# A marker transfer ahead of the last value piece, and a key load held back until it lands

## The chip, the cores and the metric

One core of a Trainium2 chip runs the kernel. The metric is the device time in microseconds (us). The profiled span is some 2 us shorter than the time. "Engine" means two things below: TensorE, VectorE and so on compute, and sixteen **DMA engines** move the data. A **landing** is the moment at which the last of a transfer's sixteen semaphore updates arrives; each DMA engine sends one.

## The reference

Two attention blocks for one decoded token, with their outputs side by side. Block A looks at the whole cache of 8192 tokens, block B at the last 2048.

```python
q = (x @ wq).reshape(B, Sq, Hq, Dh).transpose(0, 2, 1, 3)   # B=4, Sq=1, Hq=32, Dh=128
k = jnp.repeat(k_cache, rep, axis=1)                        # 8 kv heads, rep = 4
v = jnp.repeat(v_cache, rep, axis=1)                        # block B: cache[:, :, Sk - W:, :]
scores = jnp.einsum("bhqd,bhkd->bhqk", q, k) * (Dh ** -0.5)
p = softmax(scores)
o = jnp.einsum("bhqk,bhkd->bhqd", p, v)
return o.transpose(0, 2, 1, 3).reshape(B, Sq, Hq * Dh) @ wo
...
return jnp.concatenate([a, b], axis=-1)
```

The kernel has to read 184.6 MB, nearly all of it keys and values, and computes little with each byte.

## The kernel before

The work is cut into 20 units: 0 to 3 are the batches of block B, 4 to 19 are pairs of heads of block A. A unit needs 4 MB of keys and 4 MB of values, each in one of two buffers. SyncE issues nearly all loads, in program order, on one queue. Before each load it waits until the buffer is free:

```python
def kv_load(kind, u):
    ...
    if un["P"] == 1:                       # block B: keys in 2 pieces, values in NSEG = 4 pieces of 1 MB
        for q in range(NPART[kind]):
            if kind == "K":
                w = [("T", tjob_idx[(u - 2, 8 * q + 7)])] if u >= 2 else []
            else:
                w = [("otr", u - 2)] if u >= 2 else ...
            ...
            op("sp", dma(buf[:, slot, q * n:(q + 1) * n, :], src), waits=w, inc=(...))
        return
    w = [("otr", u - 2)] if kind == "V" else [("otr", u - 3)] if u >= 2 * T0P else [("T", tjob_idx[(u - 2, NJ - 1)])]
    ...                                    # block A: 4 MB in one transfer
    op("sp", lambda sp: sp.sem_inc(sem, bump), waits=w, bump=(sem, bump, None))
    op("sp", dma(buf[:, slot, :, :].rearrange("p t d -> p (t d)"), src), inc=(kind, u, 0))

kv_load("K", 0)
for u in range(1, NU + 1):
    if u < NU:
        kv_load("K", u)
    kv_load("V", u - 1)
    ...                                    # and 1 MB of output weights, from u = 6 on at every even u
for i, n in enumerate(WCH):                # eight last pieces of output weights, 128 KB each
    ...
```

So the queue holds, in order, K4, V3 (four pieces), K5, V4, K6, V5 and so on, "K5" being the keys of unit 5. TensorE's program is a part ahead of a loop, a loop of ten turns over two units each, and a tail for the last values and weights. TensorE's instructions are themselves fetched from memory in blocks.

## Time and profile before

| what | value | from |
|---|---|---|
| time | 439.17 us (439.14 to 439.53) | runs of the kernel before |
| profiled span | 437.0 us | page, first line |
| DMA queue of SyncE | 99.1% of the 16 engines' time | page, part 3 |
| TensorE busy | 84% | page, part 1 |
| VectorE, ScalarE busy | 48%, 45% | page, part 1 |
| K5: issued, landed | 98.80, 122.61 us | timeline, and the trace's semaphore updates |
| last landing | 434.43 us | trace's semaphore updates |

The full DMA row is the thing to read first: busy shares of computing engines say little in a kernel whose queue never runs empty. The lines stand in the prediction.

### The profile page before, as it was taken

The page shows a single profiled execution, that of the slowest core. Times are in us where ns is not written, and L with a number is a line of the kernel's source. Part 1 is how long each engine was busy: PE and PEld are TensorE (multiplying, and loading weights), DVE is VectorE, ACT ScalarE, POOL GpSimd, SP SyncE. Part 2 cuts the span into 40 slices and gives each one's busy share as a digit, 9 for nine tenths or more (in the row PEclk, how much of TensorE's full clock was granted, in tenths as well). Part 3 has the DMA queues.
Part 4 walks back from the last instruction along what each step waited for, and adds up shares of the span by engine and source line. Part 5 has one row for each costly group of instructions (what it writes and reads, how often), then busy time and mean ns, then how long its engine had stood idle before and what let it go on. Part 6 is the DMA issues. An engine that isn't in the chain of part 4 may idle for free.

```text
span 437.0 us, 15525 instructions
## 1 busy us (share of the span) xinstructions
PE 365.0 (84%) x7174; PEld 337.9 (77%) x7184; DVE 210.0 (48%) x406; ACT 195.0 (45%) x249; POOL 27.7 (6%) x88
## 2 busy tenths in 40 slices
PE   0168898998998959895989598969868996989996
PEld 0158897997997949795979588868868886979975
DVE  0004455664564634563456247525643563455651
ACT  1024473573653625371634254434534462536530
POOL 6100000000000000000000000000100000000000
PEclk9999999999999988999999899989996999799999
DMA  8999999999999999999999999999999999999996
GB/s 340 430 421 421 429 412 430 418 439 412 445 432 432 424 438 432 432 432 432 432 432 429 432 432 430 431 433 432 410 454 432 432 432 432 432 432 411 447 407 255
DMA packets 10996, 184.73 MB, mean 423 GB/s; under 512 B 1236, under 2 KB 2280, under 8 KB 2408
## 3 DMA queue, kind: packets, MB, share of 16 engines
q1 hardware_dynamic: 10960, 184.56, 99.1%
q8 instruction: 8, 0.13, 0.1%
q14 instruction: 4, 0.03, 0.0%
q10 hardware_dynamic: 24, 0.01, 0.0%
HBM read 184.56 MB, written 0.01 MB: 422 GB/s over the span
## 4 chain that ended last, share of the span: by engine, by line
PE 54%; DMA 40%; issue 2%; DVE 1%; SPq 1%; ACT 1%
DMA K_sb<-in_A_k_cache_dram 29%; PE KT L283 27%; PE OT L338 11%; DMA K_sb<-in_B_k_cache_dram 7%; PE SB L322 5%; PE SA L322 4%; DMA V_sb<-in_A_v_cache_dram 4%; PE KT L396 4%; PE SA L350 1%; PE KT L338 1%; SPq L566 1%; DVE oacc L404 1%; PE KT L263 1%; ACT KT_sb L299 1%; DVE OS L501 0%
## 5 line engine op out<-in xcount | busy, mean ns | idle before, releaser
L283 PE MATMUL KT<-identf,K_sb 128*128 128x128 f32 x1280 | 207.6, 296 | 44.1 <-DMA K_sb<-in_A_k_cache_dram 30.7
L299 ACT ACTIVATE KT_sb<-KT 128x1024 bf16<-128x1024 bf16 (+1 forms) x192 | 165.1, 881 | 120.6 <-PE KT L283 120.6
L283 PEld LDWEIGHTS KT<-identf,K_sb 128*128 128x128 f32 x1280 | 147.6, 150 | 49.3 <-DMA K_sb<-in_A_k_cache_dram 31.7
L299 DVE COPY KT_sb<-KT 128x512 int32<-128x512 int32 x160 | 110.5, 691 | 132.1 <-PE KT L283 130.7
L338 PE MATMUL OT<-PT,V_sb 128*128 128x64 bf16 x2560 | 78.1, 193 | 1.6 <-issue 1.1
L338 PEld LDWEIGHTS OT<-PT,V_sb 128*128 128x128 bf16 x2560 | 75.9, 98 | 1.8 <-issue 1.2
L469 ACT ACTIVATE PT<-Dt 128x512 bf16<-128x512 f32 x40 | 24.6, 630 | 84.0 <-DVE Dt L458 84.0
L322 PEld LDWEIGHTS SA<-RQc,KT_sb 128*128 128x128 bf16 x1280 | 56.9, 98 | 2.3
L322 PEld LDWEIGHTS SB<-RQc,KT_sb 128*128 128x128 bf16 x1280 | 51.1, 97 | 7.9 <-issue 4.4
L322 PE MATMUL SA<-RQc,KT_sb 128*128 128x16 bf16 x1280 | 56.4, 170 | 0.0
L322 PE MATMUL SB<-RQc,KT_sb 128*128 128x16 bf16 x1280 | 52.9, 170 | 0.0
L420 DVE TENSOR_REDUCE M<-SB 128x8 f32<-128x512 f32 (+1 forms) x20 | 13.8, 692 | 50.0 <-PE SB L322 50.0
L441 POOL PARTITION_ALL_REDUCE MB<-M1m x20 | 7.7, 387 | 334.3 <-DVE M1m L434 334.3
L396 PE MATMUL KT<-Wo_sb,OL 128*4 128x512 bf16 x80 | 18.9, 379 | 0.0
L201 PE MATMUL KT<-ident,x_sb 4*128 4x4 bf16 x8 | 0.6, 170 | 19.9 <-POOL identf L537 19.9
L201 PEld LDWEIGHTS KT<-ident,x_sb 4*128 4x128 bf16 x8 | 0.4, 112 | 20.1 <-issue 20.1
L476 DVE TENSOR_REDUCE LB<-SA 128x8 f32<-128x512 f32 (+1 forms) x20 | 13.7, 684 | 2.8 <-PE SA L350 2.8
L458 DVE TENSOR_TENSOR Dt<-SA,MBm 128x512 f32<-128x512 f32 x20 | 13.8, 692 | 0.7
L367 DVE TENSOR_TENSOR ORx<-KT,MSK 32x1024 bf16<-32x1024 bf16 x10 | 12.1, 1211 | 3.3 <-PE KT L362 3.3
L458 DVE TENSOR_TENSOR Dt<-SB,MBm 128x512 f32<-128x512 f32 x20 | 13.6, 681 | 0.0
L420 DVE TENSOR_REDUCE M<-SA 128x8 f32<-128x512 f32 (+1 forms) x20 | 13.6, 681 | 0.0
L350 PE MATMUL SA<-PT,onesb 128*128 128x128 bf16 x168 | 12.7, 218 | 0.0
(69 smaller groups left out, 118.0 us busy)
## 6 DMA issues: line engine op xcount, KB each, us to landing
K_sb<-in_A_k_cache_dram SPq DMA_DIRECT2D x15, 4096.0 KB, 22.5
V_sb<-in_A_v_cache_dram SPq DMA_DIRECT2D x15, 4096.0 KB, 30.3
K_sb<-in_B_k_cache_dram SPq DMA_DIRECT2D x8, 2048.0 KB, 23.6
V_sb<-in_B_v_cache_dram SPq DMA_DIRECT2D x16, 1024.0 KB, 18.4
V_sb<-in_B_wq_dram SPq DMA_DIRECT2D x1, 4096.0 KB, 12.5
V_sb<-in_A_wq_dram SPq DMA_DIRECT2D x1, 4096.0 KB, 21.8
Wo_sb<-in_B_wo_dram SPq DMA_DIRECT2D x4, 1024.0 KB, 11.9
K_sb<-in_A_k_cache_dram SPq DMA_DIRECT2D x2, 2048.0 KB, 17.5
```

What stands on the lines that cost most here:

```text
L283: ins = pe.transpose(out=bkf[:, pi * 128:(pi + 1) * 128], in_=K_sbf[:, slot, t0:t0 + 2, :].rearrange("p t d -> p (t d)"), identity=identf[ ...
L299: ins = e.tensor_copy(out=d, in_=r) if eng == "dve" else e.activation(out=d, in_=r, func=ACTF.Copy)
L322: ins = pe.matmul(out=stb[:, t % NTH * C:(t % NTH + 2) * C], lhsT=ktv[:, pi, :, e], rhs=RQc[:, u % 2, t // TS, e, :], start=(e == 0), stop ...
L338: ins = pe.matmul(out=otb[:, s * NW:s * NW + w], lhsT=V_sb[:, slot, t, :], rhs=PT[:, slot, t * C:t * C + w], start=(j == 0), stop=(j == n ...
L350: ins = pe.matmul(out=SA[u % 2][:, s * NM:(s + 1) * NM], lhsT=onesb[:, :], rhs=PT[:, u % 2, c0:c0 + NM], start=(i == 0), stop=(i == n - 1))
L367: return dve.tensor_tensor(out=ORx[:, :, :, :], in0=bk[0:NR, 0:128].rearrange("p (i o r) -> p r o i", o=1, r=C).broadcast_to([NR, C, C, 12 ...
L396: ins = pe.matmul(out=bk[0:Bn, 0:D], lhsT=OL[:, i, :], rhs=Wo_sb[:, i, :], start=(i == 0), stop=(i == C - 1))
L420: return dve.tensor_reduce(out=M1[:, h * n:(h + 1) * n].rearrange("p (s h) -> p s h", h=C), in_=bank[:, :].rearrange("p (s j h) -> p s h j ...
L441: return pool.partition_all_reduce(MB[:, 0:n], M1m[:, 0:n], channels=128, reduce_op=ReduceOp.max)
L458: return dve.tensor_tensor(out=Dt[:, h * NTH * C:(h + 1) * NTH * C].rearrange("p (s j h) -> p s j h", s=Sh, h=C), in0=bank[:, :].rearrange ...
L469: return act.activation(out=PT[:, u % 2, a:b], in_=Dt[:, a:b], func=ACTF.Exp, scale=scale)
L476: return dve.tensor_reduce(out=LB[:, 0:n].rearrange("p (s h) -> p s h", h=C), in_=SA[u % 2][:, 0:NSEG * NM].rearrange("p (s j h) -> p s h ...
```

## The change

A transfer that has fully passed a point of the queue can be noticed if a tiny transfer, a marker, is placed there and its semaphore is watched. The change puts such a marker (16 rows of 64 bytes, so one row for each DMA engine) ahead of the last piece of V3 and lets SyncE hold K5 back until the marker has landed. The queue then stays short at this point: K5 joins it when 1 MB is left. The values of a unit have semaphores that TensorE counts down itself, which SyncE therefore cannot watch; this explains the detour by a marker.

```diff
+        rs_sb = sb("rs_sb", [16, 32], BF16)
...
+        MARKS = (3,)
+        marked = []
+
+        def mark(u):
+            if u in MARKS:
+                op("sp", dma(rs_sb[:, :], WO[0][0:16, 0:32]), inc=("rs", u))
+                marked.append(u)
+
+        def passed():
+            return [("rs", marked.pop())] if marked else []
...
                     if kind == "K":
-                        w = [("T", tjob_idx[(u - 2, 8 * q + 7)])] if u >= 2 else []
+                        w = ([("T", tjob_idx[(u - 2, 8 * q + 7)])] if u >= 2 else []) + passed()
                     else:
                         w = [("otr", u - 2)] if u >= 2 else ...
+                        if q == NSEG - 1:
+                            mark(u)
...
-            op("sp", dma(buf[:, slot, :, :]..., src), inc=(kind, u, 0))
+            op("sp", dma(buf[:, slot, :, :]..., src), waits=passed() if kind == "K" else [], inc=(kind, u, 0))
...
             if u % 2 == 0 and tn in pieces:
                 P, q = pieces[tn]
+                mark(u - 1)
```

(The diff is cut: the new semaphore's name is also added to two lists.) With `MARKS = (3,)` the last hunk does nothing.

More of the change, by code (lines that the diff above doesn't have):

```diff
@@ L128, in bass_concat_heads__gqa_block_cached__sliding_block_cached__decode_kernel @@
                  "out0", "out1", "out2", "Tq", "Td", "Ta", "S", "PV", "Ed", "Ea", "Eq", "vs", "sub", "exp", "otr", "otp",
-                 "ocp", "Ef", "fin0", "fin1", "ar1", "SM", "msk", "pset", "setup", "pm0", "pm1", "oc", "ocB", "mkb", "perm", "rq"]
+                 "ocp", "Ef", "fin0", "fin1", "ar1", "SM", "msk", "pset", "setup", "pm0", "pm1", "oc", "ocB", "mkb", "perm", "rq", "rs"]
         sems = {n: sm("s_" + n) for n in names}
@@ L160, in sem_of @@
             return sems["vs" if t in ("max", "maxc", "sum", "rcp", "os") else t]
-        DMA_KEYS = ("K", "Kh", "KH", "V", "Vh", "VL", "WL", "x", "out", "WQ", "wo")
+        DMA_KEYS = ("K", "Kh", "KH", "V", "Vh", "VL", "WL", "x", "out", "WQ", "wo", "rs")
         plan = {e: [] for e in ("sp", "pe", "act", "dve", "pool")}
@@ L747, in kv_load @@
                 return
-            op("sp", dma(buf[:, slot, :, :].rearrange("p t d -> p (t d)"), src), inc=(kind, u, 0))
+            op("sp", dma(buf[:, slot, :, :].rearrange("p t d -> p (t d)"), src), waits=passed() if kind == "K" else [], inc=(kind, u, 0))
         for P in (1, 0):
```

## The prediction

> **What bounds the kernel now.** I read the page first (digits, queues, chain), then the SyncE timeline, the landings of single transfers, the chain in the last ten microseconds and the DMA view of short stretches. The page:
>
> ```profile
> DMA  8999999999999999999999999999999999999996
> GB/s 340 430 421 421 429 412 430 418 439 412 445 432 432 424 438 432 432 432 432 432 432 429 432 432 430 431 433 432 410 454 432 432 432 432 432 432 411 447 407 255
> ...
> q1 hardware_dynamic: 10960, 184.56, 99.1%
> ```
>
> The DMA row is full from the first slice to the last, and SyncE's queue q1 alone takes 99.1% of the time of the 16 engines. TensorE is busy for 84%, but it often waits for keys. So the transfers set the end. The steady rate is 4.19 MB in 9.71 us (spacing of landings in the trace), or 432 GB/s. SyncE's timeline around the change:
>
> ```profile
> 83.26 0.53 SPq L566 DMA_DIRECT2D K_sb<-in_A_k_cache_dram  x1
> 89.09 2.53 SPq L566 DMA_DIRECT2D V_sb<-in_B_v_cache_dram  x4
> 98.80 0.54 SPq L566 DMA_DIRECT2D K_sb<-in_A_k_cache_dram  x1
> 105.95 0.54 SPq L566 DMA_DIRECT2D V_sb<-in_A_v_cache_dram  x1
> 123.99 0.54 SPq L566 DMA_DIRECT2D K_sb<-in_A_k_cache_dram  x1
> ```
>
> These are the keys of unit 4, the four value pieces of unit 3, the keys of unit 5 (the load that the change holds back), the values of unit 4, and the keys of unit 6. The single load at 98.80, by its line:
>
> ```profile
> L566 SPq DMA_DIRECT2D K_sb<-in_A_k_cache_dram x1: 535/535/535, 98.8 to 98.8; - x1
> ...
> DMA to landing us min/median/max: 23.8/23.8/23.8
> ```
>
> It lands at 98.8 + 23.8 = 122.6, though its data need only 9.7 us: it stands 14 us in the queue. The four value pieces land at 105.44, 107.92, 110.41 and 112.89 (each time the last of 16 semaphore updates), and 112.89 + 9.72 = 122.61. There is no gap between these transfers.
>
> **The engines do not finish together.** I took the 16 updates of each transfer, as each engine sends one. At 112.89 the engines lead the slowest one by 2.07, 2.01, 1.73, 1.59, 1.38, 1.36, 1.29, 0.57, 0.41, 0.39, 0.35, 0.32, 0.26, 0.11, 0.08 and 0 us. The list hardly changes to the end: each engine runs at its own limit (a 32 KB packet takes 1.21 us, 27 GB/s), so a lead once made stays. The leads come from small jobs that one engine gets and the others don't:
>
> ```profile
> q8 instruction: 7, 0.11, 0.8%
> q14 instruction: 1, 0.01, 0.0%
> ```
>
> That is the DMA view from 20 to 75 us: seven 16 KB and one 8 KB fetches of instructions, each on one engine; another 8 KB one comes at 90.9. Nine leads are below 0.6 and seven above 1.2, which fits nine engines hit once and seven not yet. Three fetches follow later, at 159.8, 289.1 and 431.3 us. In the leads they show as one engine each: 1.31 became 0.66, about 2.05 became 1.41, and 1.63 became 0.21. All three hit engines that had a large lead, so none delayed a landing. This is what I think the change spoils.
>
> The last fetch, 431 to 433 us, and the end of the chain:
>
> ```profile
> q8 instruction: 1, 0.02, 3.5%
> ```
>
> ```profile
> 433.83 0.11 PE KT L700
> ...
> 434.43 0.11 PE SA L700
> 434.54 0.21 PE KT L700
> 434.74 0.12 PE SA L700
> 434.87 0.02 issue
> 434.89 0.41 DVE osb L704
> ```
>
> The last weight piece lands at 434.43; after that come two matmuls, a copy and the store, 2.6 us to the end of the span at 437.0. A later last landing moves the end one for one.
>
> **What the Trainium skill says.** "DMA: Bandwidth & Descriptors", Queues, rings and completion order, says that on each engine descriptors are consumed in ring order and that the semaphore increment lands only after the earlier writes of that engine. So a marker over 16 rows, one on each engine, passes an engine when it has done the first three value pieces, and its full count arrives with the slowest engine. The trace agrees: the updates of one transfer spread over the same 2.07 us that the engines are apart. The same page, Latency and other measured facts, gives about 600 ns to the first byte of such a load. In this trace the first load is issued at 0.80, its instruction takes 0.39, and its first packets start between 1.84 and 2.23, some 1.04 to 1.43 us after the issue; those first packets take 1.69 to 2.23 instead of 1.21. I use the trace. "Runtime: NRT & Kernel Launch", Instruction fetch mechanics, says the sequencer fetches 16 KiB blocks on its own DMA queue and calls the cost mostly hidden. The trace has such 16,384-byte packets on q8, but each takes about 1.05 us from one engine that carries data too.
>
> **The change part by part.**
>
> 1. It adds one transfer of 16 rows of 64 bytes. On each engine that is one packet and one semaphore write. In the trace 1 KB packets take about 46 ns and semaphore packets 9 ns, with a gap of 6: about 0.06 us on every engine, the slowest included. SyncE spends about 0.35 us more to issue it (the output stores take 0.29 to 0.37), at 91 us, 18 us before the queue needs anything: hidden. No buffer of the computation is touched.
>
> 2. It moves the key load of unit 5 from 98.80 to the marker's landing. That is 110.41 + 0.06 = 110.47; SyncE answers a semaphore about 0.02 us later (89.07 to 89.09), so about 110.5. The value load of unit 4 goes to 111.1 instead of 105.95; its turn in the queue is at 122.6, so nothing is lost. The keys of unit 6 keep their own release at 123.9. Later loads are issued 15 to 20 us ahead: unchanged.
>
> 3. When the key load is issued, the slowest engine has one piece of 1 MB before it, 2.48 us, until 112.9 + 0.06. The new packets are there at 111.5 to 111.9; so it should not run dry, or hardly. The engines with leads over about 1.3 are done with the piece at 110.9 to 111.7 and wait. To be running at full pace, an engine needs issue + 1.04 to 1.43 and then the slow first packet, 0.5 to 1.0 longer than the steady 1.21: an effective start at 112.0 to 112.9. So the seven leads of 1.29 to 2.07 shrink to between 0 and 0.9, about 0.45 in the middle. An engine at the late edge may even become the new slowest, by 0 to 0.2 us; I count 0.05.
>
> 4. The later fetches then fall on engines without the old cushion. They cost their engines 0.65, 0.64 and 1.42 us (from the leads above). With a lead of 0.45 the first two push that engine 0.2 behind the slowest, the third nearly 1.0. Three different engines are hit, so the largest counts, not the sum: 1.42 - 0.45 = 0.97. If the leads that remain are 0.9, it is 0.5; if 0, 1.4.
>
> Sum on the last landing and so on the end: 0.06 + 0.05 + 0.97 = 1.08 us. I take off a little because that engine may be fed sooner than the cold start of the program suggests: 0.85. From 439.17 this gives **440.0 us**.
>
> **The rivals.**
>
> *A: hidden anyway.* If the new descriptors come within 0.6 us of the issue and full pace follows at once, only leads over about 1.6 shrink, and the engine of the last fetch (1.59 here) keeps enough. Only the marker is left: 439.2. For it: the figure of 600 ns. Against: 1.04 us and slow first packets in this trace.
>
> *B: the whole ring runs dry.* If the answer to the marker takes over 2.5 us, all engines stop: each further microsecond costs one. With 1.5 us of extra gap and the fetches on top: about 441.5. Against it: the first packets of the first load came after 1.04 us, even cold.
>
> *C: aligned engines help.* If the engines shared a common limit, the slow ones would catch up while the fast ones wait, up to the mean lead of about 1.0: 438.2. Against it: the steady rate is the same for leaders and laggards over 300 us, and in the last 2 us, where the leaders have finished, the packets of the others still take 46 ns.
>
> *D: TensorE becomes the bound.* The keys of unit 5 land at 122.6 in both cases, and TensorE takes them up only at 123.63, so there is even 1 us of room.
>
> **Range and chances.** The centre is my sum; A marks the lower edge and a lead of zero plus a small dry spell the upper one: 439.2 to 440.9. Two per cent is 8.8 us, far beyond anything here; only a fault in my reading of the queue could reach it. Faster 0.005, within 2% 0.985, slower 0.01.
>
> **What would show it.** In the profile after: the key load of unit 5 issued near 110.5 and landing near 122.7 (issue to landing 12 instead of 23.8); the spread between the first and last update of that landing below 1.0 us instead of 2.07, and staying small; small steps of the later landings where the fetches near 160 and 289 fall; the last landing near 435.3, and most of the delay arising after 431. The prediction is wrong if the spread stays at 2 us, if the key load lands after 123.5 (the ring ran dry), or if the end moves while the landings before 431 and the fetches after it don't account for it.

## The result, and the profile after

| | before | after |
|---|---|---|
| time, median | 439.17 us (439.14 to 439.53, 4 runs) | 441.02 us (440.80 to 441.23, 4 runs) |
| profiled span | 437.0 us | 439.0 us |

The ratio is 1.004, with a 95% interval of 1.0023 to 1.0058. A ratio here is the mean time of one kernel's fast runs over that of the other's of the same rounds, so it isn't quite the ratio of the medians. The change costs 1.85 us by the medians: within 2%, but clear of noise, and just above the predicted range of 439.2 to 440.9.

The page of the changed kernel, parts 2 and 3:

```profile
DMA  8999999999999999999999999999999999999996
GB/s 341 422 423 420 426 417 428 420 448 403 403 430 430 418 443 430 433 433 427 433 433 430 430 433 433 430 428 430 422 443 442 433 430 430 430 430 414 446 412 226
...
q1 hardware_dynamic: 10992, 184.56, 98.8%
```

The row of nines shows nothing: a gap of a few tenths of a microsecond disappears in slices of 11 us. Only the rate of the eleventh slice, 403 against 445 before, is a hint. SyncE's timeline of the changed kernel (start, duration, instruction) shows the intent carried out:

```profile
88.86 1.84 SPq L567 DMA_DIRECT2D V_sb<-in_B_v_cache_dram  x3
90.74 0.66 SPq L567 DMA_DIRECT2D rs_sb<-in_A_wo_dram  x1
91.45 0.54 SPq L567 DMA_DIRECT2D V_sb<-in_B_v_cache_dram  x1
110.80 0.54 SPq L567 DMA_DIRECT2D K_sb<-in_A_k_cache_dram  x1
111.45 0.53 SPq L567 DMA_DIRECT2D V_sb<-in_A_v_cache_dram  x1
123.77 0.53 SPq L567 DMA_DIRECT2D K_sb<-in_A_k_cache_dram  x1
```

Three pieces, the marker at 90.74, the fourth piece, and K5 at 110.80 instead of 98.80. K6 is issued as before. The line of the K5 load alone:

```profile
L567 SPq DMA_DIRECT2D K_sb<-in_A_k_cache_dram x1: 535/535/535, 110.8 to 110.8; - x1
...
DMA to landing us min/median/max: 12.5/12.5/12.5
```

It lands at 123.28. A 4 MB load that follows without a gap lands 9.72 us after its predecessor, and V3 landed at 113.05, so 10.23 us lie between them: **0.51 us are lost there**. The window of 109 to 115 us, with busy time of the engines, TensorE's granted clock, share of the DMA engines and GB/s as columns (a packet counts in the window in which it starts, hence shares above 1), first before, then after:

```profile
109.00:115.00 6.00, 6.00 (x105) 5.69 (x104) 3.89 (x7) 4.21 (x5) 0.00 (x0) 1.00 1.10 466
```

```profile
109.00:115.00 6.00, 6.00 (x104) 5.68 (x103) 3.88 (x7) 3.98 (x4) 0.00 (x0) 1.00 0.94 365
```

TensorE is busy all the six microseconds in both, while the queue moves a fifth less. Summing the packets' own times from 110 to 116 us gives 96 engine-microseconds before (all that sixteen engines have) and 84 after: 12 are lost, most of them by engines that had a lead.

I then compared every landing with its counterpart of the kernel before. The delay doesn't grow evenly; it comes in steps:

| landing | delay against before | what happens there |
|---|---|---|
| last piece of V2, 93 us | +0.14 | an 8 KB fetch at 90.7; ahead of the marker |
| last piece of V3, 113.05 | +0.16 | the marker adds no more than 0.02 |
| K5, 123.28 | +0.67 | 0.51 at the marker |
| K7, 164.88 | +0.92 | an 8 KB fetch at 162.5 |
| K17, 371.66 | +0.98 | |
| first weight piece, 433.07 | +1.02 | |
| second weight piece, 434.37 | +1.97 | a 16 KB fetch at 432.1 |
| last weight piece, 436.37 | +1.94 | |

The chain of the changed kernel at its end (start, duration, what):

```profile
411.18 23.19 DMA Wl_sb<-in_A_wo_dram
434.37 0.04 issue
434.41 0.27 PE KT L701
434.69 0.11 PE SA L701
...
436.69 0.12 PE SA L701
436.81 0.02 issue
436.84 0.41 DVE osb L705
```

Before, the two products that end the chain stood at 434.54 and 434.74, and the weight pieces were mostly there ahead of them. Now the chain runs over the second weight piece, the very landing with the step of 0.95 us. In both traces the copy that ends the chain starts 0.46 us after the last landing, so the end follows the landings one for one. The same 0.46 stands in every other trace but two, e9 and e10 below.

The leads of the engines went as expected: the spread of the sixteen updates, 2.22 us at V3, is 0.72 at K5 (2.07 before) and stays below 1.05 until 432. The fetch near 432 made it 1.94 at once.

### The profile page after: what moved, and what is told of

Read it like the earlier page. It is cut to its first block, busy times and chain, and to the rows that moved or that the text cites. A ratio compares the mean times of both kernels' runs of the same rounds, so it can differ in the third digit from the quotient of the medians.

```text
span 439.0 us, 15536 instructions
## 1 busy us (share of the span) xinstructions
PE 368.8 (84%) x7184; PEld 339.4 (77%) x7184; DVE 209.8 (48%) x406; ACT 195.0 (44%) x249; POOL 27.6 (6%) x88
## 4 chain that ended last, share of the span: by engine, by line
PE 48%; DMA 42%; PEld 4%; issue 2%; SPq 1%; DVE 1%; ACT 0%; PEldq 0%
DMA K_sb<-in_A_k_cache_dram 29%; PE KT L284 24%; PE OT L339 10%; DMA K_sb<-in_B_k_cache_dram 7%; DMA Wl_sb<-in_A_wo_dram 5%; PE SB L323 4%; PE SA L323 4%; PE KT L397 3%; PEld KT L284 2%; PE SA L351 1%; SPq L567 1%; PE KT L264 1%; PEld OT L339 1%; PEld SA L323 1%; DVE oacc L405 1%
```

## The experiments

My theory: the loss has two parts. A **dry spell**: K5 is issued so late that even the slowest DMA engine waits for it. And **lost leads**: the faster engines wait for the slowest, so that a later fetch of instructions, which takes over a microsecond from one engine, no longer falls on an engine that has time to spare. Rivals: the marker itself disturbs the queue; TensorE is the cause, at the passage from the small to the large units; or the engines are realigned once and that is all.

In each trace the fetch near 91 us hits another engine and shifts all that follows by 0 to 0.65 us, ahead of the marker. So the dry spell is measured within one trace: landing of K5, minus landing of V3, minus 9.72. In the kernel before it is 122.61 - 112.89 - 9.72 = 0.00. All kernels gave correct results unless it is said otherwise. The experiments were run in four batches, each with runs of before on its own chip: e1 to e4 (before: 439.18 us), e5 to e8 (439.17), e9 to e11 (439.21, the same chip as e5 to e8) and e12 to e14 (439.21).

### e1_marker_only: the marker, but no wait

```diff
         def passed():
-            return [("rs", marked.pop())] if marked else []
+            return []
```

> The marker stays, the key load of unit 5 does not wait for it. Theory (the loss comes from holding the key load back: a dry spell of about 0.5 us, then engines without a lead): the load is issued near 98.8 again, lands near 122.7, spread of its sixteen updates about 2 us, time 439.2 us (within 0.15 of before). Rival (the marker itself, its 64-byte packets or its semaphore, disturbs the queue): time near 441.0.

Measured: 439.24 us (438.97 to 439.61), ratio 0.9998 (0.9985 to 1.0011). Dry spell 0.00, spread at K5 2.48 us. The marker itself costs nothing that can be measured; that rival falls.

### e2_hold_t5: the wait, but no marker

```diff
 # kernel before
-op("sp", dma(buf[:, slot, :, :]..., src), inc=(kind, u, 0))
+op("sp", dma(buf[:, slot, :, :]..., src), waits=[("T", tjob_idx[(4, 5)])] if kind == "K" and u == 5 else [], inc=(kind, u, 0))
```

> No marker; the key load of unit 5 waits instead for the sixth transposition of unit 4 on TensorE, which ends near 110.5 in the trace of before, so that it is issued at about the time at which the changed kernel issues it. Theory: same loss as the change, 440.5 to 441.1, landing of the load 0.3 to 0.7 us late, spread below 1 us. Rival (the marker is the cause): 439.2.

Measured: 440.16 us (439.59 to 441.20), ratio 1.0027 (1.0015 to 1.0039). The time is below my band. The load by its line:

```profile
L566 SPq DMA_DIRECT2D K_sb<-in_A_k_cache_dram x1: 535/535/535, 110.1 to 110.1; - x1
...
DMA to landing us min/median/max: 13.1/13.1/13.1
```

It was issued at 110.10, 0.7 us earlier than in the changed kernel, while the slowest engine finished V3 0.36 us later (112.94 against 112.58). That was enough: the dry spell is 0.02, no loss at K5, against what I had expected. But most of the leads went all the same (spread at K5 1.14 us, from 2.54 at V3; I had expected below 1), and at the second weight piece, just after the fetch at 431.5, the delay against before jumps from about 0.55 to 1.34; at the last one it is 1.20. So this trace happened to separate the two parts: lost leads without a dry spell cost it about 0.65 us, and no marker is needed for it. The median of the six runs lies 1.0 us over before, but the dry spells of the five without a trace are not known.

### e3_marker_2mb and e4_marker_0mb: more and less data left behind the marker

```diff
 # e3: one piece earlier                    # e4: behind the last piece
-                        if q == NSEG - 1:
+                        if q == NSEG - 2:
                             mark(u)
 # e4: mark(u) moved from ahead of the last piece's transfer to after it
```

> The marker one piece earlier, so that 2 MB instead of 1 MB of values are behind it when the key load is issued (near 108.2). Theory: the new packets come 1.3 to 2.0 us after the issue, near 109.5 to 110.2, before the fastest engine is done at 110.8; nobody runs dry, the spread stays about 2 us, time 439.2 to 439.4. Rival (any wait for a marker costs, through the sleep of SyncE or the later value load): near 441.0, or at least 440.

> The marker behind the last value piece, so that nothing is left in the queue when the key load is issued (near 113.1). Theory: all sixteen engines run dry, the load lands 12.5 us after its issue as in the changed kernel, near 125.6, which is 2.9 us late; then the last fetch adds 0.9 to 1.3. Time 443.0 to 443.6. Rival (the loss is the realignment of the engines, which is already complete in the changed kernel): about 441 again.

Measured: e3 439.39 us (439.18 to 439.76), ratio 1.0004 (0.9991 to 1.0017); e4 443.48 us (443.10 to 443.89), ratio 1.0096 (1.0081 to 1.0110). The loads by their lines, e3 and then e4:

```profile
L567 SPq DMA_DIRECT2D K_sb<-in_A_k_cache_dram x1: 535/535/535, 108.8 to 108.8; - x1
...
DMA to landing us min/median/max: 14.4/14.4/14.4
```

```profile
L567 SPq DMA_DIRECT2D K_sb<-in_A_k_cache_dram x1: 535/535/535, 113.6 to 113.6; - x1
...
DMA to landing us min/median/max: 12.3/12.3/12.3
```

Both times are as the theory expected, though in e4 not by the expected parts: the last fetch adds 0.6 us, not 0.9 to 1.3, and an 8 KB fetch at 165.5 another 0.6. With 2 MB behind the marker nothing is lost: the dry spell is -0.02, and the spread falls only from 2.59 to 2.33 us. A wait for a marker is harmless as such. With nothing behind it the dry spell is 2.76 us and the spread 0.20: all engines stood still. In these traces I set the issue of K5 against the end of the slowest engine's last data packet of V3:

| | issue of K5 ahead of that end | dry spell | spread at K5 |
|---|---|---|---|
| e3 | 4.25 us | -0.02 | 2.33 |
| e2 | 2.84 us | 0.02 | 1.14 |
| the change | 1.78 us | 0.51 | 0.72 |
| e4 | -0.65 us | 2.76 | 0.20 |

In the last two rows the two columns add up to 2.1 to 2.3 us. That is the time such a load needs here, from its issue, until it keeps every engine fed. The six other traces with this marker and wait (e6 at its first marker, e8, e10, e11, e13, e14) give 2.0 to 2.3 as well; e5, at another place, gives 3.2. To spare the leaders too, their lead of about 2 us has to be added, as e3 nearly has.

### e5_mark15 and e6_marks4: the same at another place, and at four

```diff
-        MARKS = (3,)
+        MARKS = (15,)            # e5
+        MARKS = (3, 7, 11, 15)   # e6
```

> The same marker and wait once, but at unit 15 (ahead of the 1 MB output weights, the key load of unit 17 waits), near 360 us instead of 110. Theory: a dry spell of about 0.5 us there, the fetches near 160 and 289 still harmless because the leads are still there, the one near 431 harmful: 440.6 to 441.2. Rival (the loss belongs to the passage from the small to the large units at 110 us, where TensorE is busiest): 439.2 to 439.4.

> Markers and waits at units 3, 7, 11 and 15. Theory: every one costs its own dry spell of 0.4 to 0.6 us, for in each the slowest engine too waits for its new packets; the loss of the leads comes once. So 441.0 + 3 x 0.5 = 442.5 (442.1 to 442.9). Rival (the whole loss is one realignment, later markers find the engines already together): 441.0 to 441.3.

Measured: e5 441.20 us (440.94 to 441.45), ratio 1.0044 (1.0031 to 1.0058); e6 444.35 us (443.19 to 444.62), ratio 1.0118 (1.0103 to 1.0133). In e5 the loss is as large as in the changed kernel, though the marker stands at 360 us instead of 110; the passage between small and large units is not the cause. The fetches at 160.5 and 289.1 leave hardly a step (0.1 us at most), as expected. But the dry spell is 1.42 us instead of the expected 0.5. Some 0.6 of it is common to all engines, and one engine alone is 0.78 later than the next. No fetch lies there. The packets show that this engine falls behind right at the restart: its first packet is the last to start, 2.08 us after the issue, and takes 2.03 us, and its second takes 1.66 instead of 1.21. Why it does stays open. The fetch at 433.5 then adds only 0.5.

In e6 the measure of the dry spell gives 0.26, 0.37, 0.72 and 0.59 us at the four markers. An 8 KB fetch at 281.9 falls into the third stretch and one engine is 0.32 behind the rest at its end, so about 0.4 of the 0.72 is left for the dry spell. Each marker costs one, and the rival of a single realignment is wrong. My number was too low here as well: three more markers cost 3.3 us, not 1.5. The fetches explain a part (steps of 0.6 near 160 and 1.4 near 434 in the profiled run, which was the fastest of the four); why the other three runs were over a microsecond longer than the profiled one no trace shows.

### e7_short_before and e8_short_after: a first, failed try at the fetch

```diff
 # query projection: two of the four contraction steps left out, 256 instructions less for TensorE
-                    for c in range(DC):
+                    for c in (0, DC - 1):
                         ins = pe.matmul(out=bk[:, hl * Bn:(hl + 1) * Bn], lhsT=wv[:, c, hq * DH:(hq + 1) * DH], ...)
```

> The kernel before with two of the four contraction steps of the query projection left out (wrong result on purpose): TensorE's program has 256 instructions less, so the last 16 KB fetch, near 431 us, should be gone. Theory: in the kernel before that fetch hits an engine with a lead of 1.6 us and costs nothing, so the time stays at 439.2 (438.9 to 439.4). It is the base for the next run.

> The changed kernel with the same cut (wrong result on purpose). Theory: the step of about 0.95 us near 432 disappears with the fetch, the dry spell (0.5) and the fetch near 160 (0.25) stay: 0.7 to 1.1 us over the short kernel before, 439.9 to 440.2. Rival (the step near 432 has another cause than the fetch, such as the row of small weight loads): 1.7 to 2.0 over it, near 441.0.

Measured: e7 439.47 us (439.07 to 439.68), ratio 1.0003 (0.9989 to 1.0017); e8 441.14 us (440.96 to 441.32), ratio 1.0044 (1.0030 to 1.0058). (The wrong queries still passed the comparison with the reference.) The edit missed its aim: one of the fetches before 72 us is gone, but the one near 432 is still there, at 431.8 and 432.3. It seems that the 256 instructions were exactly one 16 KB block (64 bytes each, by this count), so that all later block boundaries stayed where they were in the program. The runs say nothing about the fetch; they only repeat the loss.

### e9_notail_before, e10_notail_after and e11_refetch_after: the boundary moved to the end

```diff
 # e9 (of before), e10 and e11 (of the change): of the last values, only 2 of every 16 products are kept
-                for i in range(TC):
+                for i in range(TC) if bank is None else (0, TC - 1):
 # e11 also: the column sums of the last unit eight times over, to bring the boundary forward again
-                for s in range(NSEG):
+                for s in list(range(NSEG)) * (8 if u == L else 1):
```

> The run before this showed that cutting the program ahead of the loop by a whole 16 KB block leaves the fetch near 432 where it was, so it told nothing of the fetch. Here TensorE's tail is cut instead: of the last value product, 2 of 16 tokens in each eighth are multiplied (wrong result on purpose), which ends the program before the next 16 KB boundary. The fetch near 432 should be gone. In the kernel before it costs nothing: 438.7 to 439.4. Base for the next two.

> The changed kernel with the same cut tail (wrong result on purpose). Theory (the last microsecond of the loss is the fetch falling on an engine without a lead): no fetch near 432, no step there; the dry spell and the 8 KB fetches remain, 0.6 to 1.2 us over the cut kernel before, about 440.0. Rival (the step near 432 comes from the row of small weight loads or from TensorE's own end): 1.7 to 2.1 over it, near 441.

> The changed kernel with the cut tail, but with the eight column-sum products of the last unit done eight times over (the same values again), so that the tail crosses the 16 KB boundary once more, with few instructions on the path. Theory: the fetch is back and with it the step of about 0.5 to 1.0 us: 440.6 to 441.3. If the cut of the products was what helped and not the fetch: as the run before.

Measured: e9 440.20 us (ratio 1.0026, 1.0012 to 1.0039), e10 441.18 (1.0046, 1.0032 to 1.0059), e11 440.76 (1.0039, 1.0025 to 1.0052). By the times this failed: the base e9 is a microsecond over before, and e11 lies below e10. The landings tell it otherwise. In e9 and e10 the fetch moved to 434.1 and 434.5, when hardly any data were left, and their delays against before show no jump of more than 0.2 us in the tail: the last landing of e10 is 435.58. In e11 the fetch is back at 432.9, and the delay jumps from about 1.4 to 2.37 us at the third weight piece, which lands at 435.13. (The profiled run of e11, 441.41 us, is one of two slow ones among its five; the other three took 440.6 to 440.8 and left no trace.)

Why the times disagree shows the window of e9's last stretch, with the granted clock in the third column from the end:

```profile
432.40:436.00 3.60, 3.57 (x16) 1.88 (x16) 0.00 (x0) 0.19 (x1) 0.00 (x0) 0.50 0.29 100
```

I had taken so much work from TensorE that its granted clock fell to 0.50 and its last sixteen products took 0.21 us each instead of 0.11. They set the end in e9 and e10, not the landings: the last copy starts 1.49 and 1.40 us after the last landing there, instead of 0.46. The test had to be done again with TensorE kept busy.

### e12_busytail_before, e13_busytail_after and e14_after_again: the clean pair

```diff
 # e12 (of before), e13 (of the change): tail cut as in e9, one product more left out in each eighth, and
             pe_PV(L, c, bank=KTB[0], waits=w)
+            if c in (3, 6):          # 3 and 1 products of 128 x 512 that nobody reads
+                def keep(pe, n=3 if c == 3 else 1):
+                    for _ in range(n):
+                        ins = pe.matmul(out=KTB[1][:, :], lhsT=identf[:, :], rhs=Dt[:, 0:512], start=True, stop=True)
+                    return ins
+                op("pe", keep, waits=[("exp", L)])
```

> The kernel before with the cut tail (wrong result on purpose) and with four idle products on TensorE in it, so that TensorE keeps its full clock up to the last products. In the two runs with a cut tail its granted clock had fallen to a half there and set the end itself. Expected: granted clock 1.0 in the last stretch, the late fetch near 434 or gone, no step of the landings, 438.9 to 439.4.

> The changed kernel with the same tail (wrong result on purpose). Theory: the dry spell (0.3 to 0.5) and the 8 KB fetches (0.3 to 0.6) remain, the step of the last fetch does not: 0.7 to 1.2 us over the same tail of before, 440.0 to 440.4. Rival (the last step is not the fetch's): 1.8 to 2.0 over it, near 441.1.

> The changed kernel unaltered, on the same chip as the two runs with the kept clock, as the measure of the whole loss: 440.8 to 441.3, with the fetch near 432 and its step of 0.5 to 1.0 us.

Measured: e12 439.22 us (439.12 to 439.64), ratio 0.9998 (0.9984 to 1.0011); e13 440.42 us (440.08 to 440.85), ratio 1.0023 (1.0009 to 1.0037); e14 441.05 us (440.80 to 441.08), ratio 1.0037 (1.0023 to 1.0050). The last stretch of e12, granted clock 1.00 again:

```profile
432.40:436.00 3.60, 2.78 (x19) 1.30 (x18) 0.59 (x2) 0.37 (x1) 0.00 (x0) 1.00 0.33 111
```

The DMA view from 431 to 434.5 us has a q8 line in e14,

```profile
q8 instruction: 1, 0.02, 2.0%
```

and none in e13, where the fetch comes only at 435.8. With the fetch out of the way the loss is 440.42 - 439.22 = 1.20 us; with it, e14, 441.05 - 439.21 = 1.84. **So by the medians about 0.64 us of the loss belong to the last fetch and 1.2 to what comes earlier.** The size is rough: the means of the same runs give 0.54, with a 95% interval of some 0.1 to 0.9 us. The traces show the cause more firmly than the times: at the third weight piece, after its fetch at 432.8, the delay of e14 against before jumps from 1.57 to 2.24 (2.11 at the last piece), while that of e13 shows no jump (1.83 to 1.94 over the eight pieces). The size of the step differs from trace to trace: 0.95 in the first one of the changed kernel, 0.67 in e14, 0.45 in e8. In e13's trace the earlier part is a dry spell of 0.50 and steps of 0.30 and 0.33 at the 8 KB fetches at 163.1 and 291.0, 1.13 in sum. (Its last landing is still 1.94 us later than before, because the fetch at 90.6, ahead of the marker, cost this run 0.65. It is the slowest run of the five, 440.85 us, and in e12's trace that fetch cost 0.54.) e13 was expected at 440.0 to 440.4 and lies 0.02 above; the rival, 441.1, is ruled out. And e12 shows no cost of the fetch in the kernel before: moved away, it changes no time that these runs can measure (the interval allows 0.7 us less to 0.5 more).

No experiment pointed to a version that beats both kernels. The best variants, e1 and e3, only undo the loss.

## Why the prediction was wrong, point by point

**What bounds the kernel: right.** The delays of the landings against before are those of the end: 1.94 us at the last landing, 2.0 at the span. TensorE, rival D, is not involved; e5 shows the same loss where TensorE waits for keys anyway.

**Step 1, the marker, 0.06 us: right in kind, even smaller.** A 64-byte packet took 11 ns and a semaphore packet 9; e1 shows no loss. Its issue took SyncE 0.66 us rather than 0.35, hidden as expected.

**Step 2, the later issues: right.** K6 and all later loads are issued in time. K5 itself was issued at 110.80 rather than at 110.5: in this trace V3's third piece landed 0.19 us later than before, and the marker another 0.18 later, at 110.78.

**Step 3 failed.** It said of the slowest engine that "it should not run dry, or hardly", and counted 0.05 us; the trace has 0.51. The term that was wrong is the moment at which the slowest engine is done. I took the landing, 112.9, for it. But an update arrives some 0.45 us after its packet: the slowest engine's last data packet ended at 112.58 in the changed kernel, the landing followed at 113.05. The issue at 110.80 instead of 110.5 added to it. The time from the issue to full pace was about right, though by two errors that cancel. The first packets came 1.32 to 1.97 us after the issue, not 1.04 to 1.43; that range was misread in the trace of before, where the last three of the sixteen start 1.58, 1.60 and 2.14 us after the issue. And they took 1.40 to 2.15 us, not 1.69 to 2.23. The end of a first packet, less the steady 1.21, says when an engine runs at full pace: 1.67 to 2.40 us after the issue, where the prediction's working has 1.54 to 2.43. So with the right end of the data the prediction's own late edge would have given 110.80 + 2.43 - 112.58 = 0.65 us instead of 0.05. In the trace the last first packet ended at 114.41, where 112.58 + 1.21 = 113.79 would have kept the pace. The table of e2, e3, e4 confirms it: 2.1 to 2.3 us from the issue to full feeding, where the change leaves 1.78. That the faster engines lose their leads was right (spread 0.72 us at K5, predicted 0 to 0.9).

**Step 4, the later fetches: right in mechanism, too small.** I wrote 0.97 for all fetches together. In the trace of the changed kernel they make steps of 0.25 at 162 us and 0.95 at 432, so 1.2. I had argued that "the largest counts, not the sum". That holds as far as it goes, but the first fetch had already made another engine the slowest, and the last one took 1.54 us from its engine (1.42 was the estimate), whose lead over the slowest was 0.61. The clean pair gives 0.64 us for the last fetch in the time, and e13 0.6 for the two smaller ones: 1.2 again, though divided otherwise, because each run has its fetches on other engines.

**The deduction was wrong.** From 1.08 I took off 0.23, since an engine "may be fed sooner than the cold start of the program suggests". It was not: from the issue to full pace the warm load took 1.67 to 2.40 us, the cold one, read in the same way, 1.58 to 2.45. Without the deduction, and with 0.51 for 0.05, the same sum gives 1.54.

**In sum,** for the profiled run: 0.14 from a fetch ahead of the marker (chance of this run) + 0.02 + 0.51 + 0.25 + 0.10 (in small amounts between 165 and 433 us, not traced to anything) + 0.95 = 1.97, the delay of the second weight piece; it is 1.94 at the last.

**The rivals.** A, hidden anyway, is wrong here but true with 2 MB behind the marker (e3). B, the ring runs dry, is what happened in part, and fully in e4. C, aligned engines help, is wrong: nothing was regained anywhere.

Still open: the single late engine in e5, the longer runs of e6, and which engine is hit by which fetch. The traces don't name the engine of a packet; that a fetch falls on one engine and uses up its lead is read from the order of the sixteen updates.

## What to carry to other kernels

In this kernel the queue that was always full hid not only the latency of a load but also the differences between the sixteen DMA engines; a wait that let it run short made the fastest engines wait for the slowest, and that lead wasn't regained in the 310 us that followed. If a load must be held back, leave more in the queue than the time to feed all engines plus the spread between them (here 2.3 + 2.1 us, or about 2 MB; in e5 the first term was 3.2), and take that time from a warm load in the trace, counted to the end of the data and not to the landing. An engine that is ahead is not idle capacity: its lead is what absorbed the next small job that fell on it.

## What the Trainium skill lacked or had wrong

- "DMA: Bandwidth & Descriptors", Latency and other measured facts, gives about 600 ns to the first byte for a load issued from SyncE. Here the first packets of a 4 MB load start 1.32 to 1.97 us after its issue (change), 1.36 to 2.23 in e4, and it needs 2.0 to 2.3 us until all engines are fed (3.2 in e5). The page has no figure for this.
- The same page, Anatomy of one DMA, puts the semaphore update at about 100 ns after the receipt of the data, and the whole fixed cost at about 2 us for the GpSimd path. For loads issued by SyncE the traces show the update about 0.45 us after the start of its own packet, which directly follows the data packet; so a landing is later than the end of the engine's data by that much. The page has no figure for this path.
- No page says that the sixteen engines of one queue keep a lead over each other for hundreds of microseconds (2.0 to 2.1 us from 49 to 432 us in the kernel before, 1.88 at its last landing), nor that this lead protects the end from small transfers on single engines.
- "Runtime: NRT & Kernel Launch", Instruction fetch mechanics, calls the cost of a 16 KB block mostly hidden. It has no figure for what the fetch takes from a load that runs beside it. Here it takes about 1.1 us as a packet and 1.4 to 1.5 us from the data of one DMA engine, and in the changed kernel about 0.6 us of that reach the time (e14 against e13, by the medians).
